# Delta-rule attention and a low-rank mixer on one core: wider small products, filling products, halved weight conversions and a new written-out order

## The chip, the cores and the metric

The kernel runs on one core of a Trainium2 chip. A time is the device time of one execution in microseconds (us), from the host's launch to the end on the core; the span of a profiled execution runs from its first to its last instruction. TensorE (PE) multiplies, VectorE (DVE), ScalarE (ACT) and GpSimd (POOL) work on elements, SyncE (SP) starts transfers. Each engine takes its own instructions strictly in order and waits for the others by semaphores. The profile also tells which share of its full clock TensorE was granted.

## The reference

Attention with a state per head, 4 batches, 8 heads, 768 tokens, 48 columns, and then a mixer on 384 channels:

```python
k_n = k / (norm(k) + 1e-6)
for t in range(768):
    y[t] = q[t] @ state
    state += beta[t] * outer(k_n[t], v[t] - k_n[t] @ state)
x = y with the heads beside each other          # 4 x 768 x 384
u = x + ((x^T @ U) @ V)^T                       # rank 32, mixes tokens
out = u + relu(u @ w_ch1) @ w_ch2               # 384 -> 1536 -> 384
```

## The kernel before

Attention is cut into 12 chunks of 64 tokens for each batch and head. Two units make a batch: unit n is batch n // 2 and six of its chunks for all 8 heads, so there are units n0 to n7. For each unit:

- `turn` and `placed` (L672, L687) turn k and q on TensorE into `kq`; from n3 on `turn_blocks` does it on DVE. `products` (L700) multiplies k by k and q by k, 48 records of 64 columns for one. The k results are copied (L720), the q results masked on DVE, in two steps (L731), and the diagonal blocks are gathered.
- `norms` makes the scale `cp` from the diagonal and writes it on the diagonal of `xt` (L627, DVE).
- `blocks` inverts the diagonal blocks by substitution on DVE: for each column a product and a subtraction (L803, L809). Units n0 and n1 (`SPLIT`) and n2 (`QUARTERED`) do so for blocks of 16 and the rest for blocks of 32.
- `joins` puts the inverted blocks together on TensorE. In n0 and n1, whose blocks are of 16, it does two more products first (L860, L874) on two of the array's four quadrants, with a stationary operand of 64x64 and 16 moving columns, one product for each of 12 entries, in two halves h0 and h1. A TensorE product of this type stands as two records in the trace. The smaller products of 32x32 follow (L900 to L921).
- `prepare` (L1023, L1034) multiplies keys and values by the inverse.

`recur` then runs through the 12 chunks of a batch, one after the other: a product with the old state (L1072), a subtraction on DVE (L1085, the z), a product (L1100) and a sum on DVE (L1111, the s). `outputs` makes y beside it (L983 with the old state, L997 with z), which ACT copies to `X` (L967).

When all 12 chunks of a batch are there, `front` does the low-rank part (L1393, L1412, L1436) in three pieces of 256 tokens, and `wide` the two big products: `channels` (L1497, 384 to 1536, with a ReLU by ACT, L1462) and `narrow` (L1617, back to 384 by a scheme of seven products in place of eight, with sums on DVE). The last batch does `channels` by such a scheme too (`quick`, L1296). These wide products of earlier batches stand between the small products of later units; only ahead of the first `channels` there are none.

`load_weights` brings the mixer's weights in 14 slices and changes their number format: ACT raises a slice (`raised`, L1198), and DVE shifts it (L1212) and puts sign and tail in (L1219, L1226). Slices 0 and 1 are U and V, 2 to 7 the first weights, 8 to 13 the second ones.

The order of all this is written out by hand: each function is a generator that yields the cost of its next step, and `ORDER`, a string of names and places, says which generator goes on next. `run` follows it, so the string alone sets each engine's order, that of the transfers on SP, POOL and ACT among it. The costs and clock figures in the steps only feed the tool that wrote the string; they change nothing in the program. A step of TensorE that fills a bank of PSUM takes a free pair of banks, and the step that reads the result gives it back.

## Time and profile before

| what | us |
|---|---|
| three runs | 595.88, 597.41, 597.56 (median 597.41) |
| profiled execution | 596.68 |
| its span | 595.0 |
| TensorE busy | 560.1 (94%) |
| VectorE busy | 409.8 (69%) |
| ScalarE busy | 217.0 (36%) |
| GpSimd busy | 133.3 (22%) |
| mean granted clock of TensorE | 0.94 |

Busy time of TensorE counts from the start of a product to its modelled end, whatever the clock is. The granted clock is told for each stretch of time: at 0.50 a product streams at half speed. A window's row gives for each engine the busy time in it and, in brackets, the number of instructions; after the engines come the granted clock, the busy share of the 16 DMA engines and the bytes moved. A line of the chain of waits is a start, a duration, an engine, the tile that it writes, a source line and the number of records.

### The profile page before, as it was taken

What the parts mean: (1) busy time and instruction counts of PE and PEld (TensorE: products, weight loads), DVE (VectorE), ACT (ScalarE), POOL (GpSimd) and SP (SyncE); (2) the same over time, 40 slices, a digit from 0 to 9 for tenths busy, and PEclk for the clock granted to TensorE, in tenths of its full rate; (3) what the DMA queues carried; (4) which work ended last, traced back from release to release, by engine and by line L of the source; (5) the groups of instructions that cost most, each with busy time, mean ns of one, the idle gap of its engine ahead of it and who ended that gap; (6) DMA issues with size and microseconds to landing.
All of it is one profiled execution on the core that took longest, in us unless ns stands there. A gap on an engine that the chain in (4) does not pass through costs nothing.

```text
span 595.0 us, 23442 instructions
## 1 busy us (share of the span) xinstructions
PE 560.1 (94%) x10428; PEld 482.4 (81%) x10428; DVE 409.8 (69%) x1011; ACT 217.0 (36%) x442; POOL 133.3 (22%) x229
## 2 busy tenths in 40 slices
PE   4797987899999999999999999999999999999997
PEld 4696876688989987989889888898899778556997
DVE  3889767899999359999893389998973154122542
ACT  2558374436313442144234340234343321334000
POOL 8142133215041507312105143250110000000000
PEclk9657556999999999999999999999999999999999
DMA  9762656624041225510302035420201000000000
GB/s 141 152 154 72 216 116 146 140 70 70 3 95 22 46 42 91 99 47 17 75 2 41 11 54 93 105 58 15 68 6 37 3 2 15 26 0 1 26 28 28
DMA packets 89445, 36.23 MB, mean 61 GB/s; under 512 B 75456, under 2 KB 87104, under 8 KB 89344
## 3 DMA queue, kind: packets, MB, share of 16 engines
q1 hardware_dynamic: 80800, 24.69, 19.4%
q0 software_dynamic: 6944, 9.74, 8.2%
q8 instruction: 82, 1.34, 1.0%
q10 hardware_dynamic: 1600, 0.30, 0.3%
q14 instruction: 19, 0.16, 0.1%
HBM read 29.98 MB, written 4.72 MB: 58 GB/s over the span
## 4 chain that ended last, share of the span: by engine, by line
PE 90%; DVE 4%; issue 2%; ACT 2%; DMA 1%; SPq 0%; DVEq 0%; ACTq 0%
PE P L1617 29%; PE P L1497 25%; PE P L1296 7%; PE P L700 4%; PE P L1072 3%; PE P L983 2%; PE P L997 2%; PE P L672 2%; PE P L874 2%; PE P L1100 2%; PE P L1034 2%; PE P L1023 2%; PE P L860 2%; PE P L1412 2%; PE P L1436 1%
## 5 line engine op out<-in xcount | busy, mean ns | idle before, releaser
L1497 PE MATMUL P<-ut,w_sb 128*128 128x256 f32 x648 | 150.3, 385 | 0.9 <-ACT ut L1439 0.9
L1497 PEld LDWEIGHTS P<-ut,w_sb 128*128 128x128 f32 x648 | 119.8, 190 | 17.8 <-ACT ut L1439 1.1
L1617 PE MATMUL P<-w_sb,hs 128*128 128x192 f32 x540 | 95.8, 330 | 0.0
L1617 PEld LDWEIGHTS P<-w_sb,hs 128*128 128x128 f32 x540 | 87.4, 190 | 3.6 <-issue 1.8
L809 DVE TENSOR_TENSOR xt<-xt,prod 128x112 f32<-128x112 f32 (+21 forms) x200 | 64.6, 323 | 6.9
L803 DVE TENSOR_TENSOR prod<-gs,xt 128x112 f32<-128x112 f32 (+21 forms) x200 | 63.5, 318 | 3.6
L1537 DVE TENSOR_TENSOR X<-X,P 128x192 f32<-128x192 f32 x84 | 29.0, 348 | 49.6 <-PE P L1617 49.4
L1462 ACT ACTIVATE hs<-P 128x512 f32<-128x512 f32 x54 | 32.3, 598 | 80.0 <-PE P L1497 70.4
L967 ACT COPY X<-P 64x192 f32<-64x192 f32 x96 | 30.1, 313 | 60.7 <-PE P L997 59.6
L1617 PE MATMUL P<-w_sb,S 128*128 128x192 f32 x288 | 50.6, 330 | 0.0
L1617 PEld LDWEIGHTS P<-w_sb,S 128*128 128x128 f32 x288 | 46.6, 190 | 1.6 <-issue 1.2
L939 ACT COPY slot<-zz 32x384 f32<-32x384 f32 x64 | 32.2, 508 | 17.2 <-DVE zz L816 10.5
L555 POOL DMA_DIRECT2D slot<-in_v_dram x32 | 21.2, 665 | 66.9 <-DVE slot L747 33.4
L700 PE MATMUL P<-slot 48*64 48x64 f32 x1536 | 32.0, 235 | 4.4 <-ACT slot L687 3.7
L700 PEld LDWEIGHTS P<-slot 48*64 48x64 f32 x1536 | 28.9, 148 | 8.7 <-ACT slot L687 5.0
L1085 DVE TENSOR_TENSOR z<-slot,P 128x192 f32<-128x192 f32 x44 | 15.4, 350 | 29.2 <-PE P L1072 28.9
L946 POOL MEMSET slot<- 32x384 f32 x32 | 13.2, 413 | 96.0 <-PE P L900 52.2
L1296 PE MATMUL P<-slot,w_sb 128*128 128x384 f32 x96 | 33.2, 487 | 0.6 <-ACT slot L1365 0.6
L541 POOL DMA_DIRECT2D slot<-in_q_dram x40 | 24.6, 621 | 40.8 <-DVE slot L747 28.1
L541 POOL DMA_DIRECT2D slot<-in_k_dram x40 | 24.5, 620 | 35.5 <-DVE prod L803 18.6
L555 POOL DMA_DIRECT2D slot<-in_k_dram x44 | 29.5, 675 | 9.0 <-PE P L1100 8.7
L1305 DVE TENSOR_TENSOR slot<-slot,P 128x384 f32<-128x384 f32 x18 | 9.3, 551 | 32.4 <-PE P L1296 24.3
(153 smaller groups left out, 926.0 us busy)
## 6 DMA issues: line engine op xcount, KB each, us to landing
out_dram<-X SPq DMA_DIRECT2D x22, 192.0 KB, 2.6
w_sb<-in_moe_w_ch_dram SPq DMA_DIRECT2D x10, 384.0 KB, 5.2
slot<-in_k_dram SPq DMA_DIRECT2D x48, 72.0 KB, 3.4
slot<-in_k_dram POOLq DMA_DIRECT2D x44, 72.0 KB, 3.3
slot<-in_v_dram SPq DMA_DIRECT2D x32, 72.0 KB, 3.4
slot<-in_v_dram POOLq DMA_DIRECT2D x32, 72.0 KB, 3.6
X<-in_moe_w_ch_dram SPq DMA_DIRECT2D x6, 384.0 KB, 4.4
wide<-in_moe_w_ch_dram SPq DMA_DIRECT2D x6, 384.0 KB, 4.7
```

The lines of the kernel that those rows point to most:

```text
L541: queue.dma_start(out=blocked(n)[quarter(y % 4), j, g, :, 0:w], in_=src[b, 4 * g + 2 * j + par, hf * UC * L : (hf + 1) * UC * L, BK * low ...
L555: queue.dma_start(out=t[half(1 - g if name == "z" else g), :, to, 0:D], in_=src[b, 4 * g + s, hf * UC * L : (hf + 1) * UC * L, :].rearrang ...
L700: nc.tensor.matmul(p_g[half(g ^ (par * i)), par, c], kq[rows, c, j, 0, half(g)], kq[rows, c, j, i, half(g)], start=True, stop=True,)
L803: nc.vector.tensor_tensor(out=prod, in0=gb[:, :, j : j + 1, j + 1 :].to_broadcast([128, split, m, w]), in1=xb[:, :, 0:m, j : j + 1].to_bro ...
L809: nc.vector.tensor_tensor(out=xb[:, :, 0:m, j + 1 :], in0=xb[:, :, 0:m, j + 1 :], in1=prod, op=ALU.subtract,)
L939: nc.scalar.copy(pg[quarter(i), :, at, :, a : a + BK], cut(zc, h)[quarter(i)].rearrange("p r (c j) t -> p r c j t", j=2),)
L967: nc.scalar.copy(x[half(c % 2), c // 2, 4 * D * g : 4 * D * (g + 1)].rearrange("p (j r d) -> p r j d", r=2, d=D), states(p_y)[half(g)],)
L1296: nc.tensor.matmul(to, w, t, start=start, stop=stop, skip_group_check=True)
L1462: nc.scalar.activation(hs[:, fs[0] : fs[1] + 1 : fs[1] - fs[0]], p_f, ACTF.Relu)
L1497: nc.tensor.matmul(p_f[:, x], w(x, t), ut[:, t], start=(t == 0), stop=(t == KT - 1))
L1537: nc.vector.tensor_tensor(out=to, in0=to, in1=p, op=ALU.add)
L1617: nc.tensor.matmul(to, of[0], of[1], start=of[2], stop=of[3], skip_group_check=True)
```

## The change

- The added products of `joins` in n0 and n1 read their 16 moving columns four times (`REPEATS`), so that each writes 64 columns of which the first 16 are used. Their results lie in two banks instead of one.
- The products of `outputs` in batch 0 read their 48 columns twice (`YREPEATS`).
- Eight `filler` steps, each one product of 128x128 by 256 columns with the identity, are put into TensorE's order; nobody reads their results.
- Slices 6 to 13 of the weights are raised and converted in two halves: 8 more instructions on ACT, 24 more on DVE.
- The mask of the q products is one DVE instruction of 768 columns instead of two of 384.
- The copy of `cp` to the diagonal of `xt` goes from DVE (L627) to ACT, as a step `spread` of its own, and the substitution waits for it.
- `ORDER` is written anew throughout. Ahead of the first `channels` stand the same TensorE steps as before, and the fillers. Of n2's substitution, 5 steps that stood ahead of it stand behind it.

```diff
+    FILLERS = (0, 1, 2, 3, 4, 5, 6, 8)
     ORDER = """
...
+    REPEATS, YREPEATS = 4, 2
...
+    def spread(n):
+        yield op("act", 0.2)
+        nc.scalar.copy(
+            out=xt.rearrange("p s t -> p (s t)")[:, 0 : BK * BK : BK + 1], in_=cp[:, n % 2]
+        )
+        emitted(("spread", n), 0.06)
...
-        nc.vector.tensor_copy(
-            out=xt.rearrange("p s t -> p (s t)")[:, 0 : BK * BK : BK + 1], in_=cp[:, n % 2]
-        )
+        begin(spread(n), 2)
...
-                for par in range(2):
-                    yield op("dve", dve(384), give=[("pair", x)] if par else ())
-                    nc.vector.tensor_tensor(
-                        out=qk[:, par, :, j],
-                        in0=p_g[:, par],
-                        in1=mask_u[:, None, :].to_broadcast([128, UC, L]),
-                        op=ALU.mult,
-                    )
+                yield op("dve", dve(768), give=[("pair", x)])
+                nc.vector.tensor_tensor(
+                    out=qk[:, :, :, j],
+                    in0=p_g,
+                    in1=mask_u[:, None, None, :].to_broadcast([128, 2, UC, L]),
+                    op=ALU.mult,
+                )
...
+        yield need(("spread", n))
         for j in range(size - 1):
...
+                def products_of(x):
+                    if not lone:
+                        return one(x)[:, 0 : 12 * SB].rearrange("p (e t) -> p e t", e=12)
+                    return pair(x)[:, :, 0 : 6 * 64].rearrange("p b (e t) -> p b e t", e=6)
+
+                def at(p, y):
+                    return pair(x)[:, y // 6, 64 * (y % 6) :][:, 0 : SB * REPEATS] if lone else p[:, y]
+
+                def moving(of):
+                    return of[:, None, :].to_broadcast([L, REPEATS, SB]) if lone else of
...
                         nc.tensor.matmul(
-                            p_e[rows, y], of, zc[rows, e, SB:BK], start=True, stop=True
+                            at(p_e, y)[rows], of, moving(zc[rows, e, SB:BK]), start=True, stop=True
                         )
...
-                        nc.tensor.matmul(p_d[rows, y], of, xe[rows, y], start=True, stop=True)
+                        nc.tensor.matmul(at(p_d, y)[rows], of, moving(xe[rows, y]), start=True, stop=True)
...
+            ys = YREPEATS if b == 0 else 1
+            p_y = pair(y)[:, :, 0 : 2 * D * ys].rearrange("p g (j r d) -> p g j r d", j=2, r=ys)
...
                     nc.tensor.matmul(
-                        states(p_y)[half(g), par, j],
+                        into(g, par, j),
                         kq[half(par, D), cu, j, 1, half(g)],
-                        states(s_old)[half(par, D), g, j],
+                        over(states(s_old)[half(par, D), g, j]),
...
+        def cuts(i):
+            n = size(i)
+            return [slice(0, n)] if i < 6 else [slice(x, x + n // 2) for x in (0, n // 2)]
+
         def raised(i):
             yield need(("wide", i), ("shifted", i - 2), ("warm", 0))
-            yield op("act", act(size(i)) + 0.1)
             high = landed[i][:, :, 1].bitcast(FP32)
-            nc.scalar.mul(shape(i, scaled[i % 2][:, 0 : size(i)]), shape(i, high), 2.0 ** -112)
+            for at in cuts(i):
+                yield op("act", act(at.stop - at.start) + 0.1)
+                nc.scalar.mul(scaled[i % 2][:, at], high[:, at], 2.0 ** -112)
...
+            for at in cuts(i):
+                n = at.stop - at.start
...
+    def filler(k):
+        x = yield op("pe", 0.47, "F", take="pair", words=4, flow=0.427)
+        nc.tensor.matmul(
+            one(x)[:, 0:256], ident, ident[:, None, :].to_broadcast([128, 2, 128]), start=True, stop=True
+        )
+        free["pair"][x] = state["now"] + 0.06
```

## The prediction

> **What bounds the kernel now.** First the page: the busy tenths, to find the stretches with different limits.

> ```profile
> PE   4797987899999999999999999999999999999997
> ...
> DVE  3889767899999359999893389998973154122542
> ...
> PEclk9657556999999999999999999999999999999999
> ```

> A slice is 14.9 us. From the eighth slice on PE is full and its granted clock is 0.9 or more to the end; before it PE is fairly full too, but at 0.5 to 0.7 of its clock. Cut at the clock's steps, the windows say:

> ```profile
> core 0: us, PE busy (x) PEld busy (x) DVE busy (x) ACT busy (x) POOL busy (x), PEclk, DMA share, GB/s
> ...
> 19.00:53.00 34.00, 28.97 (x746) 27.23 (x748) 29.88 (x95) 22.69 (x45) 11.04 (x18) 0.50 0.63 150
> ...
> 60.00:87.00 27.00, 24.41 (x791) 22.99 (x793) 18.90 (x34) 15.41 (x35) 5.54 (x11) 0.50 0.56 168
> ...
> 91.00:101.00 10.00, 8.38 (x233) 7.56 (x232) 7.27 (x14) 3.80 (x8) 3.13 (x6) 0.52 0.44 113
> ...
> 116.00:150.00 34.00, 33.31 (x940) 28.22 (x940) 33.34 (x67) 15.98 (x30) 10.79 (x18) 1.00 0.35 71
> 150.00:590.00 440.00, 435.87 (x6885) 372.46 (x6876) 288.86 (x727) 136.32 (x287) 82.83 (x139) 1.00 0.19 39
> ```

> The first three rows are 71 us at half clock, with 61.8 us of PE in them and 56.1 of DVE. From 116 us, where the first wide product (L1497) starts, PE is idle for 0.7 + 4.1 us in 474: that part is its products, and only fewer of them would shorten it. So the change must win before 116 us. There the chain of waits names the products themselves:

> ```profile
> 30.42 1.49 PE P L700 x48
> 32.02 4.03 PE P L860 x72
> 36.05 1.28 PE P L874 x24
> 37.33 1.28 PE P L860 x24
> ...
> 46.78 1.36 DVE slot L636
> ...
> 53.83 2.07 DVE zz L816
> ```

> The pieces of the chain between 0 and 116 us add up to 71.0 us of PE (54.6 of it at half clock), 17.7 of DVE, 10.2 of ACT, 9.0 of issue and the rest loads. DVE bounds 44 to 56 us (the substitution of n1); elsewhere it is mostly PE at half clock (cold below, and warm at full clock).

> What sets the clock? Windows of the length of the clock's own steps (3.41 us):

> ```profile
> 8.42:11.83 3.41, 3.41 (x17) 1.00 1.34 162
> ...
> 32.31:39.14 6.83, 6.83 (x133) 0.50 0.99 234
> ...
> 56.20:59.62 3.42, 2.52 (x99) 1.00 0.02 5
> ...
> 97.16:100.58 3.42, 3.42 (x86) 0.50 0.50 142
> 100.58:103.99 3.41, 2.33 (x94) 1.00 1.06 193
> ```

> (Columns: us, PE busy and records, granted clock, which is not recorded ahead of 11.83: the first row's 1.00 is a blank.) From 32.31 to 39.14 PE is busy without a gap and stays at half clock. Its products there (L860, L874) stream 16 columns through a quarter of the array. I count for each window columns streamed times the share of the array: a full 128x256 product (two records) is 0.43 us of full streaming, from L1497, 72 records in 15.74 us. As shares of 3.41 us that gives 0.06 and 0.06 in 32.31 to 39.14; 0.37 to 0.47 in the windows after which the clock rose (8.42, 49.38, 83.51, 97.16); 0.14 to 0.26 in those after which it fell (15.25, 56.20, 86.92); and the clock stayed up after 0.36 (103.99). But 0.38 from 25.5 to 32.3 did not raise it, so the border near 0.37 is soft. Cold, the array can give no more than 0.5.

> [...] If plain busyness did decide, wider products would buy no clock at all; that is the second rival below.

> **The change part by part.**

> Repeats in the joins of n0 and n1 (L860, L874: 384 records of 64x16, now 64x64). Price now: 24 records in 1.28 us cold, 47 in 1.53 us in the warm window at 56. Bound below: L1023, also 64*64 with 64 columns but on four quadrants, does 48 in 1.29 us cold and 0.70 warm; half as many on two quadrants is the same 1.29, so nothing. Bound above: L700 (48*64 by 64) takes 1.56 cold for 48, 22% more than 1.28, and 22% of 16 joins steps of 1.28 is 4.5 us. I take 0, as L1023 has the same rows. What it buys: streaming of four times 0.06 is 0.25 cold, below the border; warm, the same products take half the time and give about 0.46, above it. So repeats hold a warm clock but do not start one.

> Repeats in the outputs of batch 0 (L983, L997: 23 steps of 16 records, 48 columns to 96). Now 0.43 us cold and 0.22 warm for 16 (chain). At 64 columns L1023 gives the same 0.43 for 16 records; half as many columns again, 0.65. So +0.22 cold or +0.11 warm a step, 23 steps: 5.0 or 2.5 us of PE. About half of these steps stand in the chain: +1.2 warm.

> Eight fillers, each a 128x256 product, two L1497 records: 0.44 warm, 0.88 cold, 3.5 to 7.0 us of PE. In the 71 us PE sits idle for 9.2, and the order puts the fillers at the start, amid the substitution of n0, behind prepare and ahead of the first front, where PE waits for DVE or ACT. I leave 0.5 us on the path; without that cover it is 3.5 to 7.

> Halves of the conversion, slices 6 to 13. From the 768- and 192-column rows of one line: L1219 0.95 and 0.35, L1226 1.03 and 0.37, L1212 0.55 and 0.24, ACT's L1198 0.92 and 0.39; the part that doesn't grow is 0.15, 0.15, 0.14 and 0.21. A second start costs 0.44 us of DVE and 0.21 of ACT a slice: 3.5 and 1.7 us. 4.5 of the 8 slices stand ahead of the first channels product: +2.0 DVE there. It also lets a z or s of the recurrence (L1085, L1111) slip in after 0.6 instead of 1.0 us; the chain has one such wait at 93.02 (0.95), so I credit -0.3.

> Masks in one step: two L731 (0.545 each) become one of 768 columns from PSUM, for which L1417 (0.95) is the nearest row: -0.14, 16 times, 5 of them in the start: -0.7 DVE. The products' bank comes free as late as before.

> The diagonal copy (L627, 0.234, 8 times, 3 in the start) moves to ACT: -0.7 DVE. ACT takes about 0.26 (L619, same shape). The substitution's first step now waits for it, with all that DVE has queued behind; L798 (0.68) stands between and covers it unless a 0.8 us copy (L687, L720) is ahead in ACT's queue: 0 to 0.8 three times; I take 0.3. DVE in the start: +2.0 - 0.7 - 0.7 = +0.6, half on the path: +0.3.

> New order. The start holds the same PE work but for the repeats and fillers; five substitution steps of n2 (about 0.6 us each) move from before the first wide product to behind it: -3.0 to 0 on the path, since DVE had been beside PE there; I take -1.0. SP and POOL: the v loads of n2 come wholly ahead of it (7 issues instead of 4, some 0.65 us each), its z loads and the last two slices' loads later. Those queues have room (POOL busy 10.6 of 41 us from 60 to 101), so nothing. Afterwards PE does the same products, with 143 changes of tiling in its order for 146: nothing.

> The clock. At full clock the chain's products take: L700 x48 0.71 for 1.56, L1023 0.70 for 1.29, L672 x6 0.82 for 1.47, so 54.6 us would be about 29.5, 25 less, were nothing else late. DVE is late next: 56.1 us of the 71 is its own work, so at most 15 goes. I take two thirds of the cold stretches as warmed. The joins of n1 and steps c6 to c11 start from a clock that is up in before too (52.8 to 59.6, 86.9 to 90.3) and fell for want of streaming (0.14, 0.26): the joins there times four and the outputs times two lift these over 0.36. n0's joins, which follow thin DVE-bound work, are the third I doubt. 25 x 2/3 is 16.7; half of it goes into waits for DVE, ACT and semaphores: -8.3.

> Sum: -8.3 + 1.2 + 0.5 - 0.3 + 0.3 + 0.3 - 1.0 = -7.3 us. The profiled execution took 596.68 (span 595.0, 1.7 around it), 0.7 under the median of 597.41; 597.4 - 7.3 is 590.1, say 590.

> **The rivals.**

> *The clock holds nearly throughout* and only DVE bounds the start: -15 + 1.2 + 0.5, 584. For it: recurrence steps stream 0.96 us warm in some 2.2 us. Against: n0's thin stage, 0.16 to 0.22 in three windows from 15.25.

> *The repeats buy no clock and cost their time: slower.* Its place is the joins and recurrence at 32 to 84 us, from the point at which a window falls under the border and stays cold; then 64-column joins give at most 0.25 and can't rise again. Half of the 5.0 us of outputs on the path, half of the 7.0 of fillers, and up to 4.5 for joins: +2.5 + 3.5 + 0 to 4.5, less 1.0 of order, 602 to 607. For it: 25.5 to 32.3 at 0.38 without a rise, and that PE is busy anyway. Against: four rises after 0.37 to 0.47, none after less.

> *The start is won and lost behind it.* DVE is busy 33.3 of 34 us from 116 to 150, and now gets the five substitution steps (3 us) and 3.5 slices of halves (1.5) more there, against 1.5 + 1.2 less in the whole remainder. If wide products then wait for weights or sums, those 4.5 us return, twice that where in-order products queue behind the late one: 594 to 600. Against: PE had other products ready there, idle 0.7 us.

> **How the numbers follow.** Forecast 0.46 (586 to 594), clock throughout 0.20 (579 to 586), cold and slower 0.18, won and lost 0.16. A measurement tells about 0.3% (1.8 us) from no change. Of the last, 0.06 ends faster, 0.06 the same, 0.04 slower. Faster: 0.46 + 0.20 + 0.06; same 0.06; slower 0.18 + 0.04. The range reaches from 579, most of the warm case, to 602, the near end of the slower one.

> **What would show it.** Granted clock near 1.0 in most windows between 19 and 101 us; L860 and L874 near 0.7 us for 24 records; the first L1497 near 108 us instead of 116; PE idle unchanged after it. Wrong if the clock rows stay at 0.50 while L860 keeps 1.3, if L983 stands long in the chain, or if PE shows waits for DVE between 110 and 150.

## The result and the profile after

The changed kernel takes 601.45 us (median of 22 runs, 595.38 to 607.5), the kernel before in the same sessions 597.48 us (22 runs, 594.7 to 600.45). The ratio is 1.0052 with an interval of 1.003 to 1.0074: slower by half a per cent, where 590 was forecast. The ratio compares the undisturbed runs alone (one run of the changed kernel, 607.5 us, stood in a slower state), so it isn't the quotient of the two medians, 1.0066. The profiled execution of the changed kernel took 601.98 us, its span 600.1. All milestones below come from one profiled execution of each kernel, which can stand 0.6% from the kernel's median (e3 and e10 below); where a few tenths of a per cent decide, the ratio is what counts.

The page of the changed kernel, the same busy tenths as before and, behind the dots, the line of the queue q8, of the kind "instruction" (packets, MB, share of time):

```profile
PE   5788768999999999999999999999998999999997
...
DVE  3899756998999549998984279888893134223542
...
PEclk9777877998999999999999999999999999999999
...
q8 instruction: 82, 1.34, 1.0%
```

The clock did rise: slices two to seven were granted 0.7 to 0.8 where the kernel before had 0.5 to 0.7. The same stretches as in the table of before, and two shorter ones (us, busy time and records of each engine, granted clock, DMA share, GB/s):

```profile
19.00:53.00 34.00, 25.90 (x783) 23.05 (x782) 30.63 (x89) 21.30 (x44) 10.71 (x18) 0.72 0.64 152
60.00:87.00 27.00, 19.73 (x792) 17.16 (x788) 19.26 (x37) 16.26 (x35) 8.03 (x14) 0.81 0.62 181
91.00:101.00 10.00, 9.36 (x311) 8.54 (x307) 5.33 (x15) 4.01 (x11) 1.17 (x2) 0.62 0.17 38
116.00:150.00 34.00, 32.05 (x849) 26.00 (x848) 30.97 (x72) 15.11 (x30) 12.34 (x22) 0.95 0.56 112
150.00:590.00 440.00, 433.52 (x6932) 371.02 (x6931) 292.81 (x719) 139.54 (x296) 81.45 (x139) 1.00 0.19 38
...
85.00:88.50 3.50, 0.00 (x0) 0.00 (x0) 1.32 (x3) 0.00 (x0) 1.26 (x2) 0.99 1.20 242
88.40:98.70 10.30, 9.42 (x198) 7.86 (x201) 3.28 (x9) 3.69 (x9) 0.00 (x0) 0.50 0.48 75
```

Read the second row against the one of before: 792 records where before had 791, in 19.7 us of TensorE instead of 24.4. The products ran faster, but no more of them were done: the time gained in the products became idle time of TensorE (7.3 us of 27 instead of 2.6). The first `channels` product starts at 115.4 us against 116.0, so nearly nothing of the gain arrives. Below, from 116 to 150 us, TensorE is idle for 1.95 us where it was 0.7, and the clock is 0.95.

What it waits for in these gaps stands in the chain of waits as "issue", which means that nothing in the profile held it back. From the chain of the changed kernel (start, duration, engine, tile, line, records; L1067 is the line that was L1034, L898 was L874, L1550 was L1497):

```profile
69.86 1.01 issue
...
84.25 0.58 PE P L1067 x38
84.84 3.80 issue
88.64 0.56 PE P L1067 x7
...
134.24 1.86 issue
136.10 1.01 PE P L898 x63
137.10 2.75 PE P L1550 x6
```

TensorE stops in the middle of a step whose operands are all there: 38 records of L1067, then nothing for 3.80 us, then the rest. In the windows above, 85.00 to 88.50 has no record of TensorE at all and 88.40 to 98.70 is at half clock. At 134.24 us it happens again, amid L898, and the six L1550 records behind it take 2.75 us where 1.56 is usual: the clock was at 0.50 again from 136.2 to 139.6 us.

These stops can be placed exactly. The queue q8 brings 82 packets of 16,384 bytes. 82 times 256 is 20,992, and the trace holds 20,981 records of TensorE (10,444 products, 10,444 loads, 93 of its sequencer); in the kernel before it is 82 packets and 20,945 records. I counted all records of TensorE (products, weight loads and its sequencer's own waits together) up to each stop of over a quarter of a microsecond; seven of the sixteen:

| kernel | a stop of "issue" ends at (us) | records so far | modulo 256 | after the last packet's landing (us) |
|---|---|---|---|---|
| before | 54.9 | 1985 | 193 | 1.52 |
| before | 58.8 | 2241 | 193 | 1.42 |
| before | 89.7 | 4033 | 193 | 1.54 |
| changed | 66.3 | 2753 | 193 | 1.48 |
| changed | 88.6 | 4033 | 193 | 1.84 |
| changed | 136.1 | 6081 | 193 | 1.55 |
| changed | 457.4 | 18369 | 193 | 1.54 |

All sixteen, which the lists of waits put down to "issue", stand at a count that leaves 193 and end 1.2 to 1.85 us after a packet has landed, while the waits for VectorE or ScalarE leave any remainder (155, 57, 88, 24, 61, ...). The profile names no cause. I read the counts so: TensorE's instructions arrive in lots of 256, one lot a packet (64 bytes each, by division), and such a stop is a lot that isn't there yet; e10, e11 and e14 put this to the test. In none of the sixteen kernels run here did two of these packets land closer than 3.2 us to each other; it was 5 us on average over the start (20 packets from 17 to 114 us in the kernel before). One step of L700, 48 records of products and 48 of loads, takes 0.71 us at full clock: a whole lot would be used up in 1.9 us. Cold it takes 1.56 us, a lot in 4.2. By this estimate the small products about keep pace with their own code at half clock, and run into the next lot's end at full clock.

In all, these stops are 6.4 us in the kernel before and 12.8 us in the changed one.

Summed up over all kernels that were run (own counts from each profiled execution: time at less than full clock before 116 us; TensorE's stops at a lot's end before and behind 116 us, those of over a quarter of a microsecond; its other idle time from 20 to 116 us; start of the first `channels` product; and from there to TensorE's end):

| kernel | cold | lot stops, start | lot stops, behind | other idle | first `channels` | to the end |
|---|---|---|---|---|---|---|
| before | 71.7 | 5.7 | 0.7 | 10.5 | 116.0 | 475.8 |
| changed | 41.0 | 8.8 | 4.0 | 10.5 | 115.4 | 481.6 |
| e1, no repeats | 64.9 | 2.8 | 3.6 | 11.2 | 113.5 | 480.8 |
| e2, no fillers | 41.0 | 9.1 | 2.8 | 13.9 | 113.9 | 479.9 |
| e3, whole slices | 41.0 | 5.2 | 1.7 | 10.9 | 110.5 | 478.8 |
| e4, old order, new code | 51.2 | 8.5 | 1.2 | 15.6 | 123.6 | 479.8 |
| e5, old order, repeats | 44.4 | 7.2 | 1.7 | 13.9 | 120.5 | 480.3 |
| e6, old order, halves | 68.3 | 6.2 | 1.8 | 12.0 | 122.5 | 479.8 |
| e7, order alone | 71.7 | 5.6 | 3.2 | 12.3 | 118.5 | 481.9 |
| e8, no tails | 41.0 | 12.2 | 4.5 | 10.2 | 115.8 | 480.3 |
| e9, before + repeats | 47.8 | 6.6 | 1.1 | 12.8 | 115.3 | 476.5 |
| e10, changed, fewer products | 34.1 | 3.7 | 2.8 | 12.1 | 108.5 | 477.7 |
| e11, lots shifted | 44.4 | 13.7 | 3.8 | 11.1 | 120.2 | 478.6 |
| e12, whole slices, no fillers | 41.0 | 8.4 | 3.4 | 15.1 | 115.1 | 480.3 |
| e13, before + repeats, fewer products | 41.0 | 3.3 | 2.3 | 17.4 | 112.5 | 478.6 |
| e14, lots shifted behind the start | 34.1 | 11.1 | 2.6 | 10.2 | 116.3 | 479.1 |

Changed against before, this is 30.7 us less cold time in the start and 3.1 us more stops there; behind it 3.3 us more stops and 3.4 us of half clock. How far one execution stands from another shows in e14: up to its first `channels` product it is the changed kernel, and yet it has 11.1 us of stops for 8.8 and 34.1 us of cold time for 41.0. Differences of that size between two rows say nothing.

### The profile page after: what moved, and what is told of

Its sections match the earlier page's. It is cut to its first block, busy times and chain, and to the rows that moved or that the text cites. A ratio compares the mean times of both kernels' runs of the same rounds, so it can differ in the third digit from the quotient of the medians.

```text
span 600.1 us, 23492 instructions
## 1 busy us (share of the span) xinstructions
PE 560.6 (93%) x10444; PEld 478.6 (80%) x10444; DVE 409.9 (68%) x1011; ACT 219.8 (37%) x458; POOL 131.7 (22%) x229
## 3 DMA queue, kind: packets, MB, share of 16 engines
q8 instruction: 82, 1.34, 1.0%
## 4 chain that ended last, share of the span: by engine, by line
PE 77%; DVE 6%; issue 3%; ACT 2%; DVEq 0%; ACTq 0%
PE P L1670 27%; PE P L1550 23%; PE P L1342 7%; PE P L709 2%; PE P L1016 2%; PE P L1105 2%; PE P L1133 2%; PE P L1030 2%; PE P L1056 1%; PE P L1067 1%; PE P L1439 1%; PE P L1458 1%; PE P L1482 1%; DVE w_sb L1174 1%; PE P L925 1%
## 5 line engine op out<-in xcount | busy, mean ns | idle before, releaser
L1550 PE MATMUL P<-ut,w_sb 128*128 128x256 f32 x648 | 151.3, 387 | 1.0 <-ACT ut L1485 0.9
L1550 PEld LDWEIGHTS P<-ut,w_sb 128*128 128x128 f32 x648 | 120.8, 191 | 18.6 <-ACT ut L1485 1.1
L1670 PE MATMUL P<-w_sb,hs 128*128 128x192 f32 x540 | 96.3, 331 | 1.5 <-issue 1.5
L1670 PEld LDWEIGHTS P<-w_sb,hs 128*128 128x128 f32 x540 | 87.3, 190 | 5.2 <-issue 4.1
L1670 PE MATMUL P<-w_sb,S 128*128 128x192 f32 x288 | 49.9, 328 | 0.0
L1670 PEld LDWEIGHTS P<-w_sb,S 128*128 128x128 f32 x288 | 46.8, 190 | 1.4 <-DVE X L1590 0.6
L971 POOL MEMSET slot<- 32x384 f32 x32 | 12.9, 411 | 134.8 <-PE P L928 108.0
L1118 DVE TENSOR_TENSOR z<-slot,P 128x192 f32<-128x192 f32 x44 | 15.4, 350 | 33.3 <-PE P L1105 33.0
L1144 DVE TENSOR_TENSOR s<-s,P 128x192 f32<-128x192 f32 x40 | 14.0, 349 | 29.6 <-PE P L1133 28.9
L545 POOL DMA_DIRECT2D slot<-in_k_dram x40 | 24.5, 618 | 42.6 <-DVE prod L812 22.3
L709 PEld LDWEIGHTS P<-slot 48*64 48x64 f32 x1536 | 27.5, 144 | 7.6 <-issue 4.0
L709 PE MATMUL P<-slot 48*64 48x64 f32 x1536 | 30.8, 231 | 2.6 <-ACT slot L696 1.4
L1670 PE MATMUL P<-w_sb,slot 128*128 128x192 f32 x180 | 30.4, 327 | 0.9 <-DVE X L1590 0.9
```

Source lines behind the costliest of these rows:

```text
L545: queue.dma_start(out=blocked(n)[quarter(y % 4), j, g, :, 0:w], in_=src[b, 4 * g + 2 * j + par, hf * UC * L : (hf + 1) * UC * L, BK * low ...
L709: nc.tensor.matmul(p_g[half(g ^ (par * i)), par, c], kq[rows, c, j, 0, half(g)], kq[rows, c, j, i, half(g)], start=True, stop=True,)
L1550: nc.tensor.matmul(p_f[:, x], w(x, t), ut[:, t], start=(t == 0), stop=(t == KT - 1))
L1670: nc.tensor.matmul(to, of[0], of[1], start=of[2], stop=of[3], skip_group_check=True)
```

## The experiments

Ratios are to the kernel before in the same session; the changed kernel's is 1.0052.

**e1: the changed kernel without the repeats.**

```diff
-    REPEATS, YREPEATS = 4, 2
+    REPEATS, YREPEATS = 1, 1
```

> The changed kernel with both repeats set to 1; order, fillers, halves and masks stay, and so does the number of instructions on every engine. Code-lot theory (the warm clock is won, but TensorE stops where its next 16,384 bytes of code are not there yet, and cools again; the repeats themselves help): cold time in the first 116 us goes from 44 back to 60 us or more, the first channels product comes 2 to 6 us later than 115.4, 603 to 607 us. Cost theory (the wider products cost TensorE more than the clock gives): 3 to 5 us faster than the changed kernel, 596 to 599.

Measured: 601.63 us, 1.0078 (1.0051 to 1.0105). Windows of e1:

```profile
19.00:53.00 34.00, 28.72 (x798) 26.39 (x802) 29.84 (x88) 21.38 (x44) 9.93 (x17) 0.56 0.63 152
60.00:87.00 27.00, 23.89 (x820) 21.70 (x822) 19.18 (x37) 17.07 (x37) 8.05 (x14) 0.57 0.58 178
```

The repeats do make the clock: without them it is 0.56 and 0.57 where the changed kernel has 0.72 and 0.81, 24 us more of cold time. And yet the time is the same within the interval, and in the second row more records are done (820 for 792). The table shows a part of what becomes of the clock: 2.8 us of stops at lot ends in e1, 8.8 with the repeats.

**e2: the changed kernel, its fillers without their product** (the step stays).

```diff
         x = yield op("pe", 0.47, "F", take="pair", words=4, flow=0.427)
-        nc.tensor.matmul(
-            one(x)[:, 0:256], ident, ident[:, None, :].to_broadcast([128, 2, 128]), start=True, stop=True
-        )
```

> The changed kernel with the eight filling products left out; each filler step still takes and gives back its bank, so everything else stays where it is. Code-lot theory: the fillers stand in idle time and hold the clock in one or two windows; without them the same time within 1.5 us or up to 3 us slower, 600 to 604. Cost theory: 8 products of 0.44 to 0.88 us partly on the path, 2 to 4 us faster, 597 to 599.

Measured: 599.43 us, 1.0029 (1.0005 to 1.0053). The cold time is 41.0 us with and without them: the fillers are not seen to hold the clock. Without them the kernel is some 0.2% faster, which is at the edge of what the intervals tell.

**e3: the changed kernel with whole slices.**

```diff
-            return [slice(0, n)] if i < 6 else [slice(x, x + n // 2) for x in (0, n // 2)]
+            return [slice(0, n)]
```

> The changed kernel with slices 6 to 13 converted whole again, each at the place of its second half (8 instructions fewer on ACT, 24 on DVE). Code-lot theory: DVE loses 3.5 us of work that is not on the path before 116 us: within 1.5 us, 600 to 603. Cost theory: the second starts are on the path of the start, where DVE works 80% of the time: 2 to 3 us faster, 598 to 600.

Measured: 597.87 us, 1.002 (0.9988 to 1.0053): the halves seem to cost 0.3%, and this kernel is not to be told from the one before. In its profiled execution (594.1, its fastest) the first `channels` product starts at 110.5 us, with only 5.2 us of lot stops ahead of it and 1.7 behind, and no cold stretch behind 116 us.

**e4, e5, e6: the order of before with all the new code but the fillers; with the repeats; with the halves.** `ORDER` is that of before, but the two mask steps of a product, which stood apart there, are one (e4) or stand right behind each other (e5, e6).

```diff
-    FILLERS = (0, 1, 2, 3, 4, 5, 6, 8)
+    FILLERS = ()
     ORDER = """
...
```

> The order of the kernel before with all new code but the fillers: repeats, halves (both halves at the place of the whole one), one mask step, diagonal copy on ACT right behind the scale. If the new order is what loses (its lots of code run out in worse places, 12.9 us of issue waits on TensorE against 6.9): the clock is warmer than in before (0.95 or more in the mean), first channels product 3 to 8 us ahead of 116.0, 590 to 595 us. If the code itself loses (cost theory): 597 us or more.

> The kernel before, its own order, with the two repeats alone (one mask of each pair is moved next to the other). It puts the clock question by itself: 16 joins steps and 23 outputs steps stream more, nothing else. Theory A (a warmer clock does not shorten the start, since DVE and TensorE's code supply are late next): cold time falls by 10 us or more from 71.7, the first channels product stays within 2 us of 116.0, 595 to 599 us. Theory B (the warmer clock does pay, and other parts of the change eat it): first channels product 3 to 6 us earlier, 591 to 594 us.

> The kernel before, its own order, with slices 6 to 13 raised and converted by halves at the place of the whole ones, and nothing else (masks as in the run beside it). Theory A (DVE is late next in the start): the second starts, 0.44 us of DVE and 0.21 of ACT a slice, stand on the path for 4 to 8 slices: 2 to 5 us slower, 599 to 602 us. Theory B (DVE has room): within 1 us of before.

Measured: e4 605.1 us, 1.0127 (1.0093 to 1.0161); e5 605.5, 1.0099 (1.0067 to 1.0132); e6 607.71, 1.0129 (1.0089 to 1.0168). These three don't say what they were made for: in them the first `channels` product waits for a mask. That the moved masks turned the rotation of the PSUM banks, and so brought this wait, is argued, not shown. From e5's timeline of TensorE, with the idle time ahead and its cause in square brackets (L738 is the mask):

```profile
120.47 2.90 PE L1548 MATMUL P<-ut,w_sb 128*128 128x256 f32 x6 [4.41 <-DVE slot L738]
```

That is 4.41 us of new idle time, where before waits 0.9 us for another result; from the first `front` product to the first `channels` product the three take 11.6 to 11.9 us for 7.8 in before, which is half or more of their loss of 6 to 8 us. A step moved by a few places in a written-out order is an edit of its own; e9 repeats e5 without it.

**e7: the new order alone**, with the old code and empty fillers.

```diff
-    REPEATS, YREPEATS = 4, 2
+    REPEATS, YREPEATS = 1, 1
```

(and whole slices, two mask steps, the copy on VectorE, no filler products)

> The new order with the old code: no repeats, fillers left out, whole slices at the place of the second half, two masks, the diagonal copy on DVE. It shows what the order itself does. Theory A: the order saves in the start (first channels product at 109 to 113, as with whole slices) and gives 4 to 6 us back behind it (476 us from there to TensorE's end in before, 479 to 482 here), as in all runs with this order: 594 to 598 us. If the loss behind 116 us comes from the code and not from the order, that stretch takes 475 to 477 us and the time is 590 to 593.

Measured: 604.85 us, 1.0089 (1.006 to 1.0118). The order alone costs 0.9%, more than the whole change. Its cold time is exactly that of before (71.7 us, and 3.4 behind). It starts `channels` at 118.5 us, and from there to the end it takes 481.9 us for 475.8: it is the order, not the new code, that loses those 6 us. The new code brings back some 40% of the loss.

**e8: the changed kernel with less work for VectorE:** the last of three conversion steps of slices 2 to 10 is left out, so the low bits of those weights are missing.

```diff
+                if 2 <= i <= 10:
+                    continue
                 nc.vector.scalar_tensor_tensor(
```

> The changed kernel without the third conversion step (the tail) of slices 2 to 10: 14 DVE instructions fewer, some 8.6 us of DVE work, most of it ahead of 120 us. It leaves out part of the weights' low bits. Theory A (with the clock up, DVE is what the start waits for): the first channels product comes 4 to 8 us earlier than 115.4, total 593 to 597 us. Theory B (TensorE and its code supply bind): less than 2 us earlier, 599 to 602.

Measured: 604.85 us, 1.0085 (1.0054 to 1.0115): not faster, rather slower. From 60 to 101 us, e8 first and then the changed kernel:

```profile
60.00:101.00 41.00, 30.34 (x1030) 26.81 (x1029) 16.41 (x40) 19.60 (x44) 8.70 (x15) 0.67 0.55 141
60.00:101.00 41.00, 31.45 (x1123) 27.31 (x1122) 24.59 (x52) 22.04 (x49) 9.20 (x16) 0.75 0.58 144
```

VectorE is busy for 16.41 us instead of 24.59, and nothing comes of it; the stops at lot ends are 12.2 and 4.5 us. So behind 60 us VectorE does not bound the start. Ahead of that e8 says nothing: the first step left out would have stood at 62 us, and from 19 to 53 us VectorE is busy for 30.33 of 34 us in e8 and 30.63 in the changed kernel.

**e9: the kernel before with the repeats and nothing else**, every step at its old place.

```diff
+    REPEATS, YREPEATS = 4, 2
```

(with the changed `joins` and `outputs` that use them)

> The kernel before with the two repeats and nothing else: order, masks, banks and the number of instructions are those of before (in the three runs above with this order, one mask had moved, the banks had turned, and the first channels product waited 4.4 us for a mask). Code-supply theory (TensorE gets its instructions in lots of 256, at best one in some 3.7 us, so dense small products can't go faster than at half clock): cold time down from 71.7 to some 45 us, first channels product at 114 to 117 as before, 594 to 599 us. Clock theory (a warm clock shortens the start): first channels product at 106 to 112, 588 to 593 us.

Measured: 595.93 us, 0.9974 (0.9951 to 0.9997). Cold time 47.8 us for 71.7, and a gain of 0.26%: 24 us of clock are worth between 0 and 3 us in the old order, too. This version is faster than both kernels, barely. The 3.7 us a lot of the expectation is not the least: two packets of q8 landed 3.38 us apart in the kernel before and 3.27 in the changed one.

**e10: the changed kernel with fewer instructions.** Of the added `joins` products of n0 and n1 every second is left out, the others read their columns eight times; half of the entries of these joins stay unwritten. Columns streamed are the same; 96 products, which stand as 192 records and as many loads, 384 instructions, are gone.

```diff
-                    return of[:, None, :].to_broadcast([L, REPEATS, SB]) if lone else of
+                    return of[:, None, :].to_broadcast([L, 2 * REPEATS, SB]) if lone else of
...
+                    if lone and y % 2:
+                        continue
```

> The changed kernel with every second added joins product of n0 and n1 left out and the others streaming 128 columns instead of 64, so that TensorE streams as long as before with 96 products (384 instructions, 1.5 lots) fewer. Every second entry gets its neighbour's numbers. Code-supply theory: 1.5 lots at 3.7 to 5 us less, the first channels product 4 to 7 us earlier than 115.4, 594 to 598 us. If streaming time or waits for DVE bind the start: within 2 us, 600 to 603.

Measured: 594.76 us, 0.9947 (0.9921 to 0.9973). Against the changed kernel this is 1.05 points, 6.3 us. The page of e10:

```profile
q8 instruction: 80, 1.31, 0.9%
```

Two lots fewer in all, 19 instead of 20 ahead of 116 us, and the first `channels` product at 108.5 us instead of 115.4. The streaming was kept, VectorE's work too; what changed is the count of instructions. How much of the 6.9 us is the products' own time can be read from the groups by line from 20 to 101 us (shape and count, busy us and mean ns of one, idle time ahead). The changed kernel:

```profile
L881 PE MATMUL P<-zz,hs 64*64 64x64 f32 x192 | 8.0, 254 | 0.6 <-DVE zz L825 0.6
...
L898 PE MATMUL P<-zz,S 64*64 64x64 f32 x192 | 6.9, 220 | 2.2 <-issue 1.7 <-ACT S L844 0.4
```

and e10:

```profile
L902 PE MATMUL P<-zz,S 64*64 64x128 f32 x96 | 6.3, 272 | 1.2 <-ACT S L844 0.8 <-DVE z L1122 0.4
L883 PE MATMUL P<-zz,hs 64*64 64x128 f32 x96 | 5.8, 271 | 0.5 <-DVE zz L825 0.5
```

14.9 us became 12.1, so 2.8 us at most are the products themselves; the stops at lot ends in the start fell by 5.1 us. So at the same columns it is the count of instructions that shortens the changed kernel's start, mostly by the stops. The 6.9 us itself is rough: e10's profiled execution (591.11) is its fastest, 3.7 us under its median.

**e11: the changed kernel with 32 tiny products (128 instructions, half a lot) behind the first filler.**

```diff
+        for y in range(32 if k == 0 else 0):
+            nc.tensor.matmul(one(x)[0:32, 256:272], ident[0:32, 0:32], ident[0:32, 0:16], start=True, stop=True)
```

> The changed kernel with 32 tiny products (128 instructions, half a lot) added behind the first filling product, while TensorE waits for the first loads. Every later end of a lot falls 128 instructions earlier in the program. Code-supply theory: the stops at the L898 joins of n2 (1.9 us at 134) and in the L1670 run at 456 us (1.5 us), which came in every run of this order, go or move to other lines; total within 4 us either way. If those stops are waits of the order itself, they stay where they are.

Measured: 603.53 us, 1.0096 (1.0063 to 1.0129). From e11's list of waits (line, cause, us in total, times, longest):

```profile
PE P L1030 <- issue: 4.7, 4, 2.7
PE P L709 <- issue: 4.2, 1, 4.2
PE P L1016 <- issue: 2.2, 1, 2.2
PE P L1067 <- issue: 1.5, 1, 1.5
```

and from that of the changed kernel:

```profile
PE P L1067 <- issue: 3.8, 1, 3.8
...
PE P L898 <- issue: 3.5, 2, 1.9
...
PE P L1670 <- issue: 1.5, 1, 1.5
...
PE P L709 <- issue: 1.1, 1, 1.1
```

The same products in the same order stop in other lines once the lots end elsewhere (and again at 193 modulo 256). L898 and L1670 are gone, and with them the half clock behind 116 us (a mean clock of 0.963 in a span of 601.9 us is 44.5 us at 0.50, and the start alone has 44.4); from the first `channels` product to the end it takes 478.6 us for 481.6. The start got 4.8 us longer, with the stop of 4.2 us in L709 in it, so that the whole is slower.

**e12: e2 and e3 together.**

```diff
-            return [slice(0, n)] if i < 6 else [slice(x, x + n // 2) for x in (0, n // 2)]
+            return [slice(0, n)]
...
-        nc.tensor.matmul(
-            one(x)[:, 0:256], ident, ident[:, None, :].to_broadcast([128, 2, 128]), start=True, stop=True
-        )
```

> The changed kernel with whole slices and without the fillers, the two parts whose removal helped alone (-0.3% and -0.2% against the changed kernel). If the two add up: 596 to 599 us, no slower than before; first channels product at 109 to 112. If they won by chance of where lots end: 599 to 603.

Measured: 600.63 us, 1.0049 (1.0028 to 1.007). The gains of e2 (0.2 points) and e3 (0.3) don't add up; together they give nothing, with 8.4 us of lot stops where e3 had 5.2. So neither can be read as a price of the fillers or the halves as such. e2 and e12 move the lots' ends by their 32 instructions; e3 leaves TensorE's instructions as they are and moves only what they wait for.

**e13: e9 with e10's edit**, to see whether code bounds the kernel before as well.

```diff
-                    return of[:, None, :].to_broadcast([L, REPEATS, SB]) if lone else of
+                    return of[:, None, :].to_broadcast([L, 2 * REPEATS, SB]) if lone else of
...
+                    if lone and y % 2:
+                        continue
```

> The kernel before in its own order, with the repeats alone as in the run that beat it (595.9, 0.9974), and of the added joins products of n0 and n1 every second left out, the others reading their columns eight times (128 columns): 192 records and as many loads, 384 instructions, fewer, with the same streaming; half of the entries of those joins stay unwritten. Theory (TensorE's instructions arrive in lots of 256 and bound the start in both kernels): another 4 to 6 us against the repeats alone, as in the changed kernel, ratio 0.987 to 0.991, first channels product at 109 to 111 us. Rival (only the new order makes lots a bound; before, the products' time at half clock was): no more than the repeats, 0.995 to 0.999, first channels product at 114 to 116 us.

Measured: 596.62 us, 0.9951 (0.9916 to 0.9985), 0.2 points better than e9, which the intervals don't secure, and no more than the rival had it; but the first `channels` product starts at 112.5 us, 2.8 us earlier than in e9 and between the two expectations. Where these went stands in its chain (L894 and L921 are steps of n2's joins, L1526 is `channels`, L1646 `narrow`):

```profile
112.53 8.04 PE P L1526 x36
...
123.09 1.32 issue
...
124.82 4.14 PE P L1526 x12
...
137.08 0.98 issue
...
143.17 2.15 PE P L1646 x12
```

and in that of the kernel before:

```profile
116.03 8.04 PE P L1497 x36
...
126.72 2.79 PE P L1497 x12
...
140.65 0.66 issue
...
143.05 2.15 PE P L1617 x12
```

The first products stand 3.5 us earlier and `narrow` starts at the same 143.1: 1.32 and 0.98 us of stops for 0.66 (+1.64), and 12 `channels` records that take 4.14 us for 2.79 (+1.35; the clock is 0.87 from 125 to 135 us, 1.00 in before), are 3.0 of the 3.5. Both stops stand at 193 modulo 256. The gain of the start was taken back by the next lots' ends and the clock that fell after the first of them.

**e14: the changed kernel with half a lot of tiny products right ahead of its first `channels` product**, so that only the lots behind the start end elsewhere.

```diff
+                for z in range(32 if b == i == y == 0 else 0):
+                    nc.tensor.matmul(p_f[0:32, 0, 0:16], ident[0:32, 0:32], ident[0:32, 0:16], start=True, stop=True)
```

> The changed kernel with 32 tiny products (128 instructions, half a lot, some 1 us) right ahead of its first channels product, so that the start stays as it is and only the ends of lots behind it move. If the place of the lots' ends costs the 5.8 us that the new order gives back behind the start: the 1.9 us stop in L898 at 134 us goes, no window behind 116 us is cold, and from the first channels product to TensorE's end it takes 478 to 480 us instead of 481.6, the 1 us of added products included; ratio to the changed kernel 0.996 to 1.000. If the order of products and sums costs it: 482 to 483 us, the stops elsewhere or not, 0.1 to 0.3% slower than the changed kernel.

Measured: 601.0 us, 1.0034 (1.0005 to 1.0064). From the first `channels` product to the end 479.1 us for 481.6, as the first theory had it, and the stop of 1.86 us in L898 is gone. From e14's timeline of TensorE:

```profile
135.80 0.38 PE L881 MATMUL P<-zz,slot 32*32 32x16 f32 x25 [1.12 <-issue]
...
137.60 0.99 PE L898 MATMUL P<-zz 32*32 32x16 f32 x96
...
139.63 1.35 PE L1552 MATMUL P<-ut,w_sb 128*128 128x256 f32 x5 [0.62 <-issue]
```

The lots that end there stop TensorE for 1.12 and 0.62 us instead, and the clock stays up: six `channels` records at 136.11 us take 1.56 us, where the changed kernel took 2.75. One part missed: a window behind 116 us is cold all the same, from 116.8 to 120.3, right after the tiny products (the first six `channels` records take 2.45 us). In the total the gain of 0.2 points is not secured by the intervals.

## Why the prediction was wrong

*The clock* (-8.3 us) is the step that failed, not in what it said of the clock but in what a clock is worth: the term was sized at -8.3 us and measured at 0 to -3. Two thirds of the cold stretches were to go; it was 43% (71.7 to 41.0 us), and e1 and e9 show that it is the repeats that do this (64.9 us cold without them, 47.8 with them alone). That fits the prediction's count of streamed columns; but the border near 0.37 is softer than my rows of before showed. In the changed kernel the clock rose after windows with 0.375 to 0.477, but also after one of 0.250. The half that I took off the gain was put down to waits for VectorE, ScalarE and semaphores, with VectorE as "late next". Behind 60 us e8 shows that it isn't late next: a third less of its work from 60 to 101 us (16.41 us for 24.59) bought nothing, with the first `channels` product at 115.8 us for 115.4. Late next there, by my reading of the stops, is the following lot of instructions: the sixth z of batch 0 ends at 84.7 us, 3.7 us ahead of the kernel before, and the seventh at 93.3, 1.4 us behind it, with the stop of 3.80 us and the half clock between them. e9 and e1 put the value of 24 us of clock at 0 to 3 us, and e10 shows that fewer instructions at the same streaming bring the first wide product forward by 6.9 us.

Ahead of 60 us the question stays open. The substitution of n1 ends at 54.6 us in the changed kernel (52.5 in e14, the same program up to there) and at 53.7 in before, with some 14 us less cold time ahead of it and only 1.4 us of stops. So the clock's gain was lost there too and not to lots; VectorE, busy for 30.63 of 34 us from 19 to 53 us, is the likely bound, as the prediction had it, but no run tests it.

The sign was in the views of before. The chain that I added up had 9.0 us of "issue" between 0 and 116 us, and I gave this no term; 5.7 us of TensorE's stops there were lots' ends. L700 at 1.56 us cold and 0.71 warm was read as a matter of the clock alone. From the list of waits of the kernel before:

```profile
PE P L1034 <- issue: 2.0, 2, 1.7
...
PE P L1023 <- issue: 1.2, 1, 1.2
...
PE P L1100 <- issue: 1.1, 1, 1.1
PE P L874 <- issue: 1.1, 1, 1.1
```

The longest five stops begin at 53.7, 58.0, 67.4, 88.0 and 94.5 us. Three of them stand in the two short warm stretches of before (52.8 to 59.6 and 86.9 to 90.3 us): they begin 0.9, 5.2 and 1.1 us after the clock had risen. The other two came at half clock, so that half clock doesn't rule them out.

*The new order* (-1.0 us) had the wrong sign. e7 gives +0.9% for it alone, about 5 us. "Afterwards: nothing" is where most of this lies: 481.6 us from the first `channels` product for 475.8. Of these 5.8 us, 3.3 are more stops at lot ends and about 1.3 the half clock from 136.2 to 139.6 us; e11 and e14, which move the lots' ends, bring back 3.0 and 2.5. The new order wins 2.0 us at the very end (108.2 us instead of 110.2 from the last z of batch 3), so some 3 us behind the start are not accounted for, and I leave their cause open. Among them can be the steps of n2 that were moved there.

*Repeats in the outputs* (+1.2) and *in the joins* (0), *fillers* (+0.5), *halves* (-0.3), *copy* (+0.3), *VectorE net* (+0.3): the first two and the last two were not measured one by one. The fillers measure +0.2 points and the halves +0.3, but e12 shows that these are not their own prices.

*The rivals.* The first, a clock that holds nearly throughout, is out: 41.0 us stayed cold. The kernel went the way that the third had named, won in the start (0.6 us) and lost behind it, but not by its mechanism. The wide products were to wait for VectorE; from 116 to 560 us its listed waits for VectorE are 2.5 us against 2.1 before, and the stops for code 4.0 against 0.7. The second, that the repeats buy no clock, is refuted by e1. Its 602 to 607 stood nearer to 601.45 than the third's 594 to 600, by luck and not by its mechanism.

*What would show it:* the clock is 0.72 from 19 to 53 us and 0.81 from 60 to 87, not near 1.0; the first `channels` product came at 115.4 us and not near 108; idle time behind it did not stay unchanged. Each of the three tells the miss apart by place.

*The range* reached to 602 for the sake of the slower rivals, and 601.45 lies just in it, by the mechanism of neither.

## What to carry to other kernels

In a kernel with many small products like these, count instructions besides columns: each stands as two records of the product and two of its load, and 384 instructions fewer at the same columns (e10) took 6.3 us off. Here packets of 16,384 bytes never landed closer than 3.2 us to each other, about 13 ns an instruction if each brings 256; from 60 to 87 us the clock rose from 0.50 to 0.81 and TensorE's idle time from 2.6 to 7.3 us, which I read as mostly the wait for code. "issue" in the chain of waits, amid a step whose operands are there, is the place to look; the remainder of the instruction count (193 modulo 256 in these kernels), with a packet's landing 1.2 to 1.85 us ahead, told such a stop from the others. In a kernel with a written-out order, undo an edit with every other step left at its place; a mask moved by a few steps cost more here than all that was to be measured.
